# An FFT layer and a squared-relu FFN on one core: row d = 128 by a DMA, and P-Q+N moved to odd steps

## The chip, the core and the metric

The kernel runs on one NeuronCore of a Trainium2 chip. The metric is device time in microseconds for one execution. Before the change the median of three runs is 607.77 us (607.44 to 608.54). The engines are TensorE (PE in the profile, its weight loads PEld), VectorE (DVE), ScalarE (ACT), GpSimd (POOL) and SyncE (SP).

## The reference

```python
# x: 8 x 3008 x 256, w_in: 256 x 2048, w_out: 2048 x 256
X = np.fft.fft(x, axis=1)
X = np.fft.fft(X, axis=2)
a = X.real                      # 24064 rows of 256
h = np.maximum(a @ w_in, 0.0)
out = (h * h) @ w_out
```

## The kernel before

**Two outputs from one column.** The input is real, so the kernel transforms over the sequence only for the frequencies k up to half the sequence. For each such k it has a cosine part zc and a sine part zs (128 rows d, one column per k). With gh[:, 0] and gh[:, 1] (w_in after the transform over d) the hidden layer at k is relu of P+Q and the one at -k is relu of P-Q plus a small term N, where P comes from zc and Q from zs. N comes from one row alone, d = 128, which is kept in row 0 of zs: N for hidden unit f is that row times a number g2n[f].

**Windows and steps.** The 12040 columns are cut into 25 windows of up to 512 columns (`wins`; from window 6 on all have 512, the last, window 24, has 360). A window has 8 steps (`NST`), and a step makes 2 x 128 of the 2048 hidden units for all columns of the window, plus half (k) and minus half (-k), into h2. In the steps of window w also run: the second layer of window w-1 (16 matmuls of 256 columns per step, L687; the output copy osb, L702, comes in every odd step), the transform matmuls of the columns of window w+1 (`z_steps`, L572, spread over the steps lo to hi-1), and pieces of the input folds for a later batch (`at`, `post`: d_even, n_cos, d_odd, n_sin, even, away, odds, back, load, and the late pieces fold8, fold16, nyq8).

**Two forms of a step.** A *plain* step has four matmuls into a PSUM tile ph (`pq`, L829 and L830), the relu of the plus half on ScalarE (`first`, L861), the second-layer matmuls, two more matmuls with gh[:, 2] that turn P+Q into P-Q+N in place (`turn`, L852), and the relu of the minus half on ScalarE. VectorE squares both halves in one instruction (`power`, L868, 128x2048).

A *P-Q+N* step (the steps named in `diff`) saves the two `turn` matmuls: `cosines` (L838, two matmuls) makes P; VectorE computes t2 = N - 2P (`twice`, L842, scalar_tensor_tensor, called STT below); the second-layer matmuls run; `sines` (L847, two matmuls) makes P+Q in place and must wait for t2, since it writes the bank that t2 reads; ScalarE makes the relu of the plus half; VectorE adds t2 and ph with a saturating custom instruction (L859), which is the relu of the minus half. This instruction waits for ScalarE's relu of the same step. ScalarE squares the plus half (L872, issued after the relu of the next step), VectorE the minus half (L868, 128x1024).

**N.** n2 holds N for one P-Q+N step. `spread_nyq` brings row 0 of zs to all 128 partitions as zn: a matmul with a selector (`sel`, ones in row 0) into PSUM and a copy by ScalarE (L781, L782). `nyq_rows` makes n2 on GpSimd: per step two tensor_scalar instructions of 128x512 (L790). zn has two buffers. n2 has three (`wp`, tag w16), so the fourth set in order waits until the STT that reads the first has run.

**Order.** Everything is in an order written out by hand; each engine works its own instructions off in that order. Squares are not issued when they are ready: `keep` puts them in a list, and `settle` issues the list in the next step, after that step's `pq` or `twice`. `plus` does so for ScalarE's squares, after the relu of the next step. `held` keeps the transform's VectorE part (`apart`, L601) back, so that it does not come ahead of an STT. PSUM tile ph has two buffers, so step s+2 waits until both relus of step s have read theirs.

Before the change the P-Q+N steps are 0, 2, 4 and 6 in windows 6, 7, 11, 12, 14, 15, 17, 18 and 20 to 24; 2, 4 and 6 in windows 8, 10, 13, 16 and 19 (where the folds run in every step); 0 and 2 in window 9; 4 and 6 in windows 4 and 5. These are 73 steps. The row for window w+1 is spread in step `hi` of window w (5 or 6), and GpSimd makes the rows in that step and the next ones.

Of the kernel before, what the change touches and what calls it, by code (L numbers as in the profile page):

```python
# [9 lines left out]
F32 = mybir.dt.float32  # L10
F16 = mybir.dt.float16
I32 = mybir.dt.int32
AF = mybir.ActivationFunctionType
# [3 lines left out]
P = 128  # L17
# [3 lines left out]
def rev_dim(ap, i):  # L21

    dims = [list(d) for d in ap.ap]
    step, cnt = dims[i]
    dims[i] = [-step, cnt]
    return bass.AP(tensor=ap.tensor, offset=ap.offset + step * (cnt - 1), ap=dims)
# [3 lines left out]
def kernel(  # L30
# [14 lines left out]
    nc = tc.nc  # L45
    B, S, D = x.shape
# [33 lines left out]
    NW = len(wins)  # L80

    def win_of(col):
        return max(w for w in range(NW) if wins[w][0] <= col) if col < TOT else NW
# [5 lines left out]
    col_of = {}  # L89
# [11 lines left out]
    const = ctx.enter_context(tc.tile_pool(name="const", bufs=1))  # L101
# [12 lines left out]
    ps_z = ctx.enter_context(tc.tile_pool(name="ps_z", bufs=2, space=bass.MemoryType.PSUM))  # L114
# [35 lines left out]
    def load_rows(i):  # L150

        b, t = bs[i], xs[i]
        o = b * S * D
        if b == 0:
            nc.gpsimd.dma_start(out=t[0:1, 0, R - 1, :], in_=bass.AP(tensor=x.tensor, offset=x.offset + o, ap=[[D, 1], [1, D]]))
        if b + 1 == B:
            nc.gpsimd.dma_start(
                out=t[1:2, 2, :, :].rearrange("p c d -> p (c d)"),
                in_=bass.AP(tensor=x.tensor, offset=x.offset + o + (S - R) * D, ap=[[XW, 1], [1, XW]]))
# [156 lines left out]
    for i in (1, 0):  # L316
        nc.gpsimd.tensor_scalar(out=perm[i], in0=prow_i, scalar1=float(P - 1 - i), scalar2=None, op0=ALU.is_equal)
    nc.gpsimd.dma_start(out=wout16, in_=moe_w_out.rearrange("(c p) o -> p c o", p=P))
    sel = const.tile([P, P], F16, name="sel")
    nc.gpsimd.memset(sel, 0.0)  # L320
    nc.gpsimd.memset(sel[0:1, :], 1.0)
    pick = const.tile([P, 1], F16, name="pick")
    nc.gpsimd.memset(pick, 0.0)
    nc.gpsimd.memset(pick[0:1, :], -2.0)
# [213 lines left out]
    def zwin(w):  # L538
        if w not in zc:
            zc[w] = zp.tile([P, WN], F16, name="zc", tag="zc")  # L540
            zs[w] = zp.tile([P, WN], F16, name="zs", tag="zs")
        return zc[w], zs[w]

    held = {"on": False, "jobs": []}

    def let_go():
        jobs, held["jobs"] = held["jobs"], []
        for j in jobs:
            j()
# [81 lines left out]
    def run(*jobs):  # L631
        for j in jobs:
            j()
# [82 lines left out]
    def spread(jobs, i, n):  # L716
        return jobs[len(jobs) * i // n : len(jobs) * (i + 1) // n]
# [7 lines left out]
    NST = NFC // 2  # L725
    at_of = {w: [[] for _ in range(NST)] for w in range(NW)}
    post_of = {w: [[] for _ in range(NST)] for w in range(NW)}
    diff = {w: (0, 2, 4, 6) if w > 5 else (4, 6) for w in range(4, NW)}

    def put(w, s, i, name, *k, d=at_of):  # L730
        d[w][s].append(lambda: folds[i][name](*k))

    def late(w, s, i, *st):
        at_of[w][s].append(lambda: run(*[folds[i]["late"][k] for k in st]))

    def make(i):
        folds[i] = fold_steps(i)

    for i in range(2, B):
        b0 = (win_of(col_of[i, 0]) + win_of(col_of[i - 1, 1])) // 2 - 1  # L740
        tight = b0 - 2 in [(win_of(col_of[j, 0]) + win_of(col_of[j - 1, 1])) // 2 - 1 for j in range(2, i)]
        near = i == 2 or tight
        at_of[b0 - 1][0].append(lambda i=i: make(i))
        at_of[b0 - 2][7].append(lambda i=i: load_rows(i))
        put(b0 - 1, 5 if near else 2, i, "d_even", 0)
        put(b0 - 1, (6 if tight else 7) if near else 4, i, "d_even", 1)
        put(b0 if i == 2 else b0 - 1, 0 if i == 2 else 7 if near else 6, i, "n_cos")
        put(b0, 0, i, "d_odd", 0)
        put(b0, 1, i, "d_odd", 1)
        put(b0, 2, i, "n_sin")  # L750
        put(b0, 3, i, "even")
        put(b0, 4, i, "away")
        put(b0, 5, i, "odds")
        put(b0, 6, i, "back")
        put(b0, 6, i, "nyq", d=post_of)
        put(b0, 7, i, "load")
        for k, s in enumerate((3, 5, 6, 6)):
            late(b0 + 1, s, i, k)
        late(b0 + 2, 0, i, 4)
        if b0 > 5:  # L760
            diff[b0] = (2, 4, 6)
        if tight:
            diff[b0 - 1] = (0, 2)
    n2s = {}
    BIG = 3.0e38
    kept = []
    plus = []

    def settle():
        for k in kept:  # L770
            k()
        kept.clear()
        let_go()

    zns = {}

    def spread_nyq(wt):
        wn1 = wins[wt][1]
        zn = zns[wt] = znp.tile([P, WN], F16, name="zn", tag="zn")
        pn = ps_z.tile([P, 512], F32, name="pn", tag="pz")  # L780
        nc.tensor.matmul(pn[:, 0:wn1], sel, zwin(wt)[1][:, 0:wn1], start=True, stop=True)  # L781
        nc.scalar.activation(zn[:, 0:wn1], pn[:, 0:wn1], AF.Copy, bias=0.0, scale=1.0)  # L782

    def nyq_rows(wt, steps):
        wn1 = wins[wt][1]
        for s in steps:
            n2 = n2s[wt, s] = wp.tile([P, 2, WN], F32, name="n2", tag="w16")
            for a in range(2):
                fc = 2 * s + a
                nc.gpsimd.tensor_scalar(out=n2[:, a, 0:wn1], in0=zns[wt][:, 0:wn1], scalar1=g2n[:, fc : fc + 1], scalar2=1.0, op0=ALU.mult, op1=ALU.mult)  # L790

    old = None
    for w in range(NW):
# [1 line left out]
        h2 = h2p.tile([P, NFC, 2 * WN], F16, name="h2", tag="h2")  # L795
        zcw, zsw = zwin(w)

        lo, hi = int(any(win_of(col_of[i, 1]) == w + 1 for i in range(2, B))), NST - 3 if 0 in diff.get(w + 1, ()) else NST - 2
        at, post = at_of[w], post_of[w]
        if w == 1:  # L800
            fj = fold_jobs(1)
# [6 lines left out]
        elif w == 3:  # L808
# [4 lines left out]
            lo, hi = 3, NST - 1  # L813
        elif w == win_of(col_of[1, 1]) - 1:
            for st in range(5):
                at[min(st, 3)] += folds[1]["late"][st : st + 1]
            lo, hi = 4, NST - 1
# [36 lines left out]
        def relu(s, sg):  # L854
            h = h2[:, 2 * s : 2 * s + 2, sg * wn : (sg + 1) * wn]
            if sg:
                h = rev_dim(h, 2)
            if sg and s in t2s:
                nc.vector._custom_dve(TENSOR_ADD_SAT, out=h, in0=t2s[s][:, :, 0:wn], in1=phs[s][:, :, 0:wn], s0=BIG, s1=0.0)  # L859
            else:  # L860
                nc.scalar.activation(h, phs[s][:, :, 0:wn], AF.Relu, bias=0.0, scale=-1.0)  # L861

        def keep(*k):
            kept.append(lambda p=power: p(*k))

        def power(s, a, b, h2=h2, wn=wn):
            h = h2[:, 2 * s : 2 * s + 2, a * wn : b * wn]
            nc.vector.tensor_tensor(h, h, h, op=ALU.mult)  # L868
# [5 lines left out]
        def first(s):  # L874
            relu(s, 0)
            run(*plus)
            plus.clear()

        def others(s):
            for j in at[s]:  # L880
                j()
            for j in spread(f2, s, NST):
                j()
            for j in post[s]:
                j()
            if s == lo:
                zl[:] = [j for zu, part, h in zj for j in zu(part, h)]
            if s >= lo:
                for j in spread(zl, s - lo, hi - lo) if s < hi else []:
                    j()  # L890

        def nyq(s):
            if w + 1 in diff and hi < NST - 1:
                if s == hi:
                    spread_nyq(w + 1)
                    nyq_rows(w + 1, diff[w + 1][0:1])
                elif s == hi + 1:
                    nyq_rows(w + 1, diff[w + 1][1 : 2 if s < NST - 1 else None])
                elif s == hi + 2:
                    nyq_rows(w + 1, diff[w + 1][2:])  # L900
            if s == 0 and w in diff and w not in zns:
                spread_nyq(w)
                nyq_rows(w, diff[w])

        def quad(p):
            ph = phs[p] = ps_h.tile([P, 2, 512], F32, name="ph", tag="psh")
# [57 lines left out]
                keep(s1, int(s1 == NST - 1), 2)  # L964
            gh_nyq()
        for s in range(NST) if w > 1 else ():
            held["on"] = s + 1 in diff.get(w, ()) or (s + 1 == NST and 0 in diff.get(w + 1, ()))
            if s in diff.get(w, ()):
                cosines(s)
                twice(s)  # L970
                settle()
                others(s)
                sines(s)
                first(s)
                relu(s, 1)
                keep(s, 1, 2)
                plus.append(lambda s=s, p=power_act: p(s))
                nyq(s)
                continue
            pq(s)  # L980
            settle()
            first(s)
            if s == NST - 1:
                power(s, 0, 1)
            others(s)
            nyq(s)
            turn(s)
            relu(s, 1)
            keep(s, int(s == NST - 1), 2)
        if 0 not in diff.get(w + 1, ()):  # L990
            held["on"] = False
            settle()
        old = (w, h2)
    for j in ffn2_steps(*old, tail=True):
        j()
# [30 lines left out]
```

## Time and profile before

| | |
|---|---|
| median of three runs | 607.77 us |
| the profiled execution | 607.33 us, span 605.5 us |
| PE busy | 591.2 us, 98% |
| DVE busy | 490.1 us, 81% |
| ACT busy | 462.8 us, 76% |
| POOL busy | 213.6 us, 35% |
| selector matmul, L781 | 21, 379 ns each as the profile models it |
| copy to zn, L782 | 21, 616 ns mean with 512 columns |
| rows on POOL, L790 | 146, median 692 ns, up to 2444 |
| square of one half, L868 128x1024 | 107, mean 767 ns |
| square of both halves, L868 128x2048 | 73, mean 1284 ns |

All times are of one execution, counted from the start of its span. [...] Window 12 starts at 282.05, window 15 at 354.38, window 18 at 427.22, window 20 at 475.32, window 23 at 547.63, the last at 570.38.

### The profile page before, as it was taken

How to read it: one execution, taken by the hardware profiler on the slowest of the kernel's cores; microseconds unless marked ns; L12 is line 12 of the kernel's file. 1: busy time of each engine (PE TensorE's matmuls, PEld its weight loads, DVE VectorE, ACT ScalarE, POOL GpSimd, SP SyncE). 2: the span in 40 equal slices, each digit the busy share in tenths (PEclk: the TensorE clock that was granted, in tenths of full speed). 3: DMA queues.
4: the chain of work that ended last, by engine and by line, in shares of the span. 5: the costliest groups of instructions: out<-in, count | busy, mean ns of one | idle time of the engine just before them, and what ended most of it. 6: DMA issues, size and time to landing. Idle time of an engine off the chain costs nothing.

```text
span 605.5 us, 11294 instructions
## 1 busy us (share of the span) xinstructions
PE 591.2 (98%) x4449; PEld 427.9 (71%) x4449; DVE 490.1 (81%) x593; ACT 462.8 (76%) x634; POOL 213.6 (35%) x249
## 2 busy tenths in 40 slices
PE   7899999999999999999999999999999999999997
PEld 3457786776777777777777767777677777777786
DVE  8787656987998878979889799888988988777760
ACT  6697777968888787877787878787777787878762
POOL 8320223245504506365045451363431522513300
PEclk9999999999999999999999999999999999999999
DMA  8945321127111361271113711146112311111112
GB/s 150 155 90 136 115 71 34 39 94 150 52 49 40 114 140 52 77 166 48 52 37 109 146 53 36 40 125 134 44 30 86 88 35 39 51 46 38 54 57 69
DMA packets 36524, 47.52 MB, mean 78 GB/s; under 512 B 4215, under 2 KB 30327, under 8 KB 36471
## 3 DMA queue, kind: packets, MB, share of 16 engines
q0 software_dynamic: 9344, 22.14, 17.9%
q1 hardware_dynamic: 26899, 24.44, 13.5%
q8 instruction: 35, 0.57, 0.4%
q10 hardware_dynamic: 228, 0.21, 0.1%
q14 instruction: 18, 0.15, 0.1%
HBM read 33.63 MB, written 27.84 MB: 102 GB/s over the span
## 4 chain that ended last, share of the span: by engine, by line
PE 87%; DVE 9%; ACT 2%; issue 1%; POOL 0%; DVEq 0%; POOLq 0%; ACTq 0%
PE po L687 49%; PE ph L852 8%; PE ph L829 7%; PE ph L830 7%; PE ph L847 5%; PE ph L838 5%; PE pz L572 4%; DVE h L868 3%; DVE t L842 2%; DVE h L859 2%; DVE xy L491 1%; PE pn L781 1%; ACT h L923 1%; ACT h L861 0%; DVE m L243 0%
## 5 line engine op out<-in xcount | busy, mean ns | idle before, releaser
L687 PE MATMUL po<-wout,h 128*128 128x256 f16 (+1 forms) x3024 | 362.3, 273 | 0.0
L861 ACT ACTIVATE h<-ph 128x1024 f16<-128x1024 f32 (+3 forms) x311 | 295.5, 993 | 79.0 <-PE ph L847 59.1
L687 PEld LDWEIGHTS <-h 128*128 128x128 f16 (+1 forms) x3024 | 296.8, 98 | 72.0
L790 POOL TENSOR_SCALAR n<-zn,g2n 128x512 f32<-128x512 f16 (+2 forms) x146 | 144.2, 1002 | 256.3 <-ACT zn L782 248.4
L868 DVE TENSOR_TENSOR h<-h 128x1024 f16<-128x1024 f16 (+6 forms) x216 | 203.2, 951 | 30.0 <-ACT h L861 27.5
L859 DVE CUSTOM_DVE_ANT_0 h<-t,ph 128x1024 f16<-128x1024 f32 x67 | 81.7, 1220 | 31.6 <-ACT h L861 31.5
L842 DVE SCALAR_TENSOR_TENSOR t<-ph,n 128x1024 f32<-128x1024 f32 (+2 forms) x73 | 87.7, 1202 | 23.4 <-PE ph L838 22.1
L829 PE MATMUL ph<-zc,gh 128*128 128x512 f16 (+3 forms) x238 | 87.4, 368 | 0.4 <-ACT h L923 0.3
L830 PE MATMUL ph<-zs,gh 128*128 128x512 f16 (+3 forms) x238 | 87.4, 368 | 0.0
L872 ACT ACTIVATE h<-h 128x1024 f16<-128x1024 f16 (+2 forms) x73 | 76.5, 1048 | 0.0
L852 PE MATMUL ph<-zs,gh 128*128 128x512 f16 (+3 forms) x238 | 68.1, 368 | 0.2 <-ACT h L861 0.2
L702 ACT ACTIVATE osb<-po 128x512 f32<-128x512 f32 (+3 forms) x95 | 55.5, 589 | 10.6 <-PE po L687 9.7
L847 PE MATMUL ph<-zs,gh 128*128 128x512 f16 (+2 forms) x146 | 42.7, 374 | 1.4 <-DVE t L842 1.2
L838 PE MATMUL ph<-zc,gh 128*128 128x512 f16 (+2 forms) x146 | 42.8, 375 | 0.4 <-DVE h L859 0.4
L830 PEld LDWEIGHTS <-gh 128*128 128x128 f16 x238 | 23.2, 98 | 25.7 <-issue 0.9
L829 PEld LDWEIGHTS <-gh 128*128 128x128 f16 x238 | 23.2, 97 | 25.0
L577 ACT ACTIVATE es<-pz 128x376 f32<-128x376 f32 (+1 forms) x32 | 14.9, 486 | 16.4 <-PE pz L572 16.3
L852 PEld LDWEIGHTS <-gh 128*128 128x128 f16 x238 | 22.3, 98 | 6.2 <-issue 0.3
L838 PEld LDWEIGHTS <-gh 128*128 128x128 f16 x146 | 14.3, 98 | 17.2 <-issue 0.6
L456 POOL DMA_DIRECT2D scr<-ev x8 | 4.9, 616 | 58.3 <-DVE ev L452 52.5
L466 POOL DMA_INDIRECT rb<-scr,idx_r x16 | 18.2, 1140 | 4.9 <-issue 4.9
L132 POOL DMA_INDIRECT xo<-in_x_dram,idx_r x15 | 16.3, 1090 | 4.5 <-issue 4.3
(145 smaller groups left out, 368.5 us busy)
## 6 DMA issues: line engine op xcount, KB each, us to landing
out_dram<-osb SPq DMA_DIRECT2D x77, 128.0 KB
xo<-in_x_dram POOLq DMA_DIRECT2D x7, 768.0 KB
scr<-ev POOLq DMA_DIRECT2D x8, 390.0 KB, 2.9
rb<-scr POOLq DMA_DIRECT2D x16, 130.0 KB
out_dram<-osb SPq DMA_DIRECT2D x12, 94.0 KB
w<-in_moe_w_in_dram POOLq DMA_DIRECT2D x2, 512.0 KB
wout<-in_moe_w_out_dram POOLq DMA_DIRECT2D x1, 1024.0 KB, 11.9
out_dram<-osb SPq DMA_DIRECT2D x8, 75.0 KB
```

Of the source, the lines that this page charges most:

```text
L687: nc.tensor.matmul(po[0:m, j * D : (j + 1) * D], h2[:, fc, q : q + m], wout16[:, fc, :], start=(fc == 0), stop=(fc == NFC - 1))
L790: nc.gpsimd.tensor_scalar(out=n2[:, a, 0:wn1], in0=zns[wt][:, 0:wn1], scalar1=g2n[:, fc : fc + 1], scalar2=1.0, op0=ALU.mult, op1=ALU.mult)
L829: nc.tensor.matmul(ph[:, a, 0:wn], gh[:, 0, f0 : f0 + P], zcw[:, 0:wn], start=True, stop=False)
L830: nc.tensor.matmul(ph[:, a, 0:wn], gh[:, 1, f0 : f0 + P], zsw[:, 0:wn], start=False, stop=True)
L838: nc.tensor.matmul(ph[:, a, 0:wn], gh[:, 0, f0 : f0 + P], zcw[:, 0:wn], start=True, stop=True)
L842: nc.vector.scalar_tensor_tensor(out=t2[:, :, 0:wn], in0=phs[s][:, :, 0:wn], scalar=-2.0, in1=n2s[w, s][:, :, 0:wn], op0=ALU.mult, op1=ALU ...
L847: nc.tensor.matmul(phs[s][:, a, 0:wn], gh[:, 1, f0 : f0 + P], zsw[:, 0:wn], start=False, stop=True, skip_group_check=True)
L852: nc.tensor.matmul(phs[s][:, a, 0:wn], gh[:, 2, f0 : f0 + P], zsw[:, 0:wn], start=False, stop=True, skip_group_check=True)
L859: nc.vector._custom_dve(TENSOR_ADD_SAT, out=h, in0=t2s[s][:, :, 0:wn], in1=phs[s][:, :, 0:wn], s0=BIG, s1=0.0)
L861: nc.scalar.activation(h, phs[s][:, :, 0:wn], AF.Relu, bias=0.0, scale=-1.0)
L868: nc.vector.tensor_tensor(h, h, h, op=ALU.mult)
L872: nc.scalar.activation(h, h, AF.Square, bias=0.0, scale=1.0)
```

## The change

Row d = 128 is no longer spread by a matmul and a copy. ScalarE's DMA queue copies row 0 of zs, inside SBUF, to the 128 partitions of zn: one descriptor list of 128 times 1 KB. The selector and its two memsets go.

The P-Q+N steps become 1, 3, 5 and 7 where they were 0, 2, 4 and 6; 1 and 3 in window 9; 1, 3 and 5 in the last window. Windows 4, 5, 8, 10, 13, 16 and 19 keep theirs. There are 72 such steps instead of 73. Where step 7 is one, its plus half is squared on VectorE in that step (not on ScalarE), and its minus half in step 1 of the next window (`defer`).

The row is issued in step 4 or 5 (`hi`), where the transform matmuls of the next window have ended: these now take the steps 0 to hi-1. GpSimd makes one step's rows in each following step (one step later still in windows 5, 8, 10, 13, 16 and 19, where `back` is issued in step 6), and what is left in step 0 of the next window. d_even moves from steps 2 and 4 to 3 and 5, and the late fold pieces move from steps 3, 5, 6, 6 and 0 of the next window to 3, 4, 5, 5 and 6.

```diff
-    sel = const.tile([P, P], F16, name="sel")
-    nc.gpsimd.memset(sel, 0.0)
-    nc.gpsimd.memset(sel[0:1, :], 1.0)
...
-    diff = {w: (0, 2, 4, 6) if w > 5 else (4, 6) for w in range(4, NW)}
+    diff = {w: (4, 6) if w < 6 else (1, 3, 5) if w == NW - 1 else (1, 3, 5, 7) for w in range(4, NW)}
+    backs = []
...
+        backs.append(b0)
+        late(b0 + 1, 3, i, 0)
+        late(b0 + 1, 4, i, 1)
+        for k in (2, 3):
+            late(b0 + 1, 5, i, k)
+        late(b0 + 1, 6, i, 4)
+        put(b0 - 1, 5 if near else 3, i, "d_even", 0)
+        put(b0 - 1, (6 if tight else 7) if near else 5, i, "d_even", 1)
...
-            diff[b0 - 1] = (0, 2)
+            diff[b0 - 1] = (1, 3)
...
-        pn = ps_z.tile([P, 512], F32, name="pn", tag="pz")
-        nc.tensor.matmul(pn[:, 0:wn1], sel, zwin(wt)[1][:, 0:wn1], start=True, stop=True)
-        nc.scalar.activation(zn[:, 0:wn1], pn[:, 0:wn1], AF.Copy, bias=0.0, scale=1.0)
+        row = zwin(wt)[1][0:1, 0:wn1]
+        nc.scalar.dma_start(out=zn[:, 0:wn1], in_=bass.AP(tensor=row.tensor, offset=row.offset, ap=[list(row.ap[0]), [0, P], [1, wn1]]))
...
-        lo, hi = int(any(win_of(col_of[i, 1]) == w + 1 for i in range(2, B))), NST - 3 if 0 in diff.get(w + 1, ()) else NST - 2
+        lo, hi = 0, NST - 4 if 1 in diff.get(w + 1, ()) else NST - 3 if w + 1 in diff else NST - 2
...
+            if w + 1 in diff:
+                k = s - hi - int(w in backs)
                 if s == hi:
                     spread_nyq(w + 1)
+                elif s > hi and k > 0:
+                    nyq_rows(w + 1, diff[w + 1][k - 1 : k])
+            if s == 0 and w in diff:
+                nyq_rows(w, [q for q in diff[w] if (w, q) not in n2s])
...
                 settle()
+                if s == 1:
+                    run(*defer)
+                    defer.clear()
...
+                if s == NST - 1:
+                    power(s, 0, 1)
+                    relu(s, 1)
+                    defer.append(lambda p=power, s=s: p(s, 1, 2))
+                else:
+                    relu(s, 1)
+                    keep(s, 1, 2)
+                    plus.append(lambda s=s, p=power_act: p(s))
```

More of the change, by code (lines that the diff above doesn't have):

```diff
@@ L744 @@
         at_of[b0 - 2][7].append(lambda i=i: load_rows(i))
-        put(b0 - 1, 5 if near else 2, i, "d_even", 0)
-        put(b0 - 1, (6 if tight else 7) if near else 4, i, "d_even", 1)
+        backs.append(b0)
[6 more added lines that the diff above has]
+        put(b0 - 1, (6 if tight else 7) if near else 5, i, "d_even", 1)
         put(b0 if i == 2 else b0 - 1, 0 if i == 2 else 7 if near else 6, i, "n_cos")
@@ L756 @@
         put(b0, 7, i, "load")
-        for k, s in enumerate((3, 5, 6, 6)):
-            late(b0 + 1, s, i, k)
-        late(b0 + 2, 0, i, 4)
         if b0 > 5:
@@ L767 @@
     plus = []
+    defer = []
     def settle():
@@ L892, in nyq @@
         def nyq(s):
-            if w + 1 in diff and hi < NST - 1:
+            if w + 1 in diff:
+                k = s - hi - int(w in backs)
                 if s == hi:
                     spread_nyq(w + 1)
[L896 to L903, printed above, removed]
+                elif s > hi and k > 0:
+                    nyq_rows(w + 1, diff[w + 1][k - 1 : k])
+            if s == 0 and w in diff:
+                nyq_rows(w, [q for q in diff[w] if (w, q) not in n2s])
         def quad(p):
@@ L966 @@
         for s in range(NST) if w > 1 else ():
-            held["on"] = s + 1 in diff.get(w, ()) or (s + 1 == NST and 0 in diff.get(w + 1, ()))
+            held["on"] = s + 1 in diff.get(w, ())
             if s in diff.get(w, ()):
@@ L974 @@
                 first(s)
-                relu(s, 1)
-                keep(s, 1, 2)
-                plus.append(lambda s=s, p=power_act: p(s))
+                if s == NST - 1:
[6 more added lines that the diff above has]
+                    plus.append(lambda s=s, p=power_act: p(s))
                 nyq(s)
@@ L981 @@
             settle()
+            if s == 1:
+                run(*defer)
+                defer.clear()
             first(s)
@@ L989 @@
             keep(s, int(s == NST - 1), 2)
-        if 0 not in diff.get(w + 1, ()):
-            held["on"] = False
-            settle()
+        settle()
         old = (w, h2)
```

## The prediction

> **What bounds the kernel now.** I read the page's first part, then the chain of work in order of time, then the timeline of single engines around a step, then the places where TensorE was late.
>
> ```profile
> span 605.5 us, 11294 instructions
> PE 591.2 (98%) x4449; PEld 427.9 (71%) x4449; DVE 490.1 (81%) x593; ACT 462.8 (76%) x634; POOL 213.6 (35%) x249
> ```
>
> TensorE (PE) is busy 98% of the span. A modelled busy time could hide waits, so the chain is the better witness (columns: start, length, piece):
>
> ```profile
> 249.93 1.20 PE po L687 x11
> 251.13 0.21 PE pn L781
> 251.34 0.43 PE ph L852 x2
> 251.78 0.43 PE ph L838 x2
> 252.21 1.75 PE po L687 x16
> ```
>
> The matmuls stand end to end: 0.216 us for one of 512 columns, 1.75 for the sixteen of the second layer. So a P-Q+N step lasts 0.43 + 1.75 + 0.43 = 2.61 us, a plain step 0.87 + 1.75 + 0.43 = 3.05. The selector matmul (L781) is one link of this chain: whatever leaves TensorE here shortens the run.
>
> **Removed and added on TensorE.** The selector runs 21 times: 19 with 512 columns, one with 448, one with 360. 19 x 0.216 + 0.19 + 0.15 = 4.44 us gone, all on the chain. The last window has P-Q+N in three steps instead of four; such a step spares two matmuls of 360 columns, so 2 x 0.15 = 0.30 us come on. Elsewhere the number of such steps is unchanged.
>
> **Old waits that go.** Step 0 no longer has the form that waits for VectorE. What it cost is read in window 15 (step 0 from 354.38):
>
> ```profile
> 354.38 0.59 PE L838 MATMUL ph<-zc,gh 128*128 128x512 f16 x2
> 354.81 1.91 PE L687 MATMUL po<-wout,h 128*128 128x256 f16 x16
> 357.31 0.59 PE L847 MATMUL ph<-zs,gh 128*128 128x512 f16 x2 [0.59 <-DVE t L842]
> ```
> ```profile
> 354.31 1.81 DVE L868 TENSOR_TENSOR h<-h 128x1024 f16<-128x1024 f16 x2
> 356.05 1.21 DVE L842 SCALAR_TENSOR_TENSOR t<-ph,n 128x1024 f32<-128x1024 f32 x1
> ```
>
> The sines (L847) start 2.50 us after the second layer instead of 1.75: 0.75 lost. The same two rows give 0.17, 0.24, 0.74 and 0.24 in windows 7, 12, 18 and 21 (at 162, 284, 430, 503): 2.14 us together. VectorE came late because two squares of the window's last step lie ahead of P-Q+N there. In the new order step 0 has none, so these waits go; what is late next is step 7.
>
> **The new window boundary.** In 12 windows (6, 7, 11, 12, 14, 15, 17, 18, 20 to 23) step 7 becomes P-Q+N, and the square of its plus half must go on VectorE at once, ahead of the second relu. A light step in window 23 gives the times; let X be the start of the sines, 544.15:
>
> ```profile
> 544.78 1.94 ACT L861 ACTIVATE h<-ph 128x1024 f16<-128x1024 f32 x2 [1.02 <-PE ph L847]
> 547.55 0.60 ACT L702 ACTIVATE osb<-po 128x512 f32<-128x512 f32 x1
> 548.03 1.03 ACT L861 ACTIVATE h<-ph 128x1024 f16<-128x1024 f32 x1
> ```
> ```profile
> 545.84 1.22 DVE L859 CUSTOM_DVE_ANT_0 h<-t,ph 128x1024 f16<-128x1024 f32 x1 [0.48 <-ACT h L861]
> 547.09 1.30 DVE L868 TENSOR_TENSOR h<-h 128x1024 f16<-128x1024 f16 x2
> ```
>
> The relu starts at X + 0.63 and the custom add follows its end by 0.03. In step 7 the output copy (osb, odd steps) lies ahead: it starts 0.31 after the last second-layer matmul starts, X + 0.20, and the next activation 0.49 later, X + 0.69. Relu to X + 1.72; square from X + 1.75, next instruction 0.61 later (half of the x2 row); custom add X + 2.36 to X + 3.58. It frees the PSUM buffer that step 1 of the next window wants, and TensorE starts 0.055 after it (in window 20 at 482.08 to 482.14), X + 3.63. TensorE is there at X + 0.43 + 0.87 + 1.75 + 0.43 = X + 3.48. Lost: 0.16 us per boundary, 1.9 in all. This is the low end.
>
> GpSimd adds to it. There are three n2 buffers, so the third set of rows for the next window waits for step 7's STT (L842), which ends at X - 0.26; then two tensor_scalars run beside VectorE's squares. What such a meeting costs stands above: in the 354.31 row the two squares take 1.81 instead of 1.30, while GpSimd has
>
> ```profile
> 354.31 2.37 POOL L790 TENSOR_SCALAR n<-zn,g2n 128x512 f32<-128x512 f16 x2
> ```
>
> The square that comes into a running tensor_scalar waits for its end and then needs 0.55. Here the first tensor_scalar waits behind the full square of step 6 (X - 0.34 to X + 0.88) and ends near X + 1.43, the second near X + 2.10; the new square arrives at X + 1.75 and ends at X + 2.65 instead of X + 2.44. So 0.16 + 0.20 = 0.36 us per boundary, 12 x 0.36 = 4.3. I take this, because the buffer order makes them meet in every one of the 12.
>
> [...]
>
> **ScalarE.** 21 zn copies go (0.49 us each from one start to the next), 21 DMA issues come. Issues on this queue are in the tail, two in 0.81 us:
>
> ```profile
> 598.11 0.81 ACTq L667 DMA_DIRECT2D out_dram<-osb  x2
> ```
>
> I take 0.35. In step 4, counted from its first matmul: relu to 2.0, Square to 3.0, issue to 3.4, while relu of the minus half could start at 3.24. It is 0.2 us late; its square is not started before 4.9, its PSUM buffer not wanted before 5.66. Cost nothing; the cover is 0.4 us on VectorE's side, 1.2 on TensorE's. The issue also waits for VectorE's last part of zs (L601), which lies a step earlier. The high end is SyncE's row, 15 issues in 21.3 us, where the longest took 4.7; 14 of 311 took over 0.9. At that rate one of 21 costs 1 to 3 us.
>
> **Landing of the row.** Nearest: scr, 2.9 us; farthest: the indirect load, 11.4. The first rows are wanted in step 1 of the next window, about 11.7 us after the issue; two sets need 2.8 to 3.8. Hidden by 5 us at 2.9; at 11.4 late by 1 to 3 in each window (the less likely end: that row moves far more bytes).
>
> **The rest that moves.** The z steps end in step 3 instead of 4 or 5: same matmuls, their copies on ScalarE (0.49) now beside steps 0 to 3, whose plain ones lose the output copy (0.49). d_even moves a step later (0.97 on VectorE, two copies on ScalarE), each still in a P-Q+N step. fold8, fold16 and nyq8 come by step 6; 0.7 us in step 5 ends at 3.7 after the cosines, the relu that the custom add waits for at 3.9. GpSimd issues two scratch DMAs and two gathers in step 6, now ahead of the rows: 5 us of queue, rows wanted later than that. x loads and SyncE's stores keep their steps. The deferred square runs in step 1 and is wanted in step 4. One loss: n_cos (0.89) ahead of step 7's STT in windows 7, 12, 15 and 18 makes it about 0.1 late each, 0.4 in all; I set it against the 0.53 in window 20 that goes (next paragraph).
>
> **Sum.** -4.44 + 0.30 - 2.14 + 4.3 = -1.98 us on the profiled execution's 607.33 (span 605.5 and 1.8 around it): 605.35. The median of the runs, 607.77, stands 0.44 above that execution; so 605.8.
>
> **Rivals.** One, slower: GpSimd's burst starves the square. It has happened:
>
> ```profile
> 476.38 4.03 POOL L790 TENSOR_SCALAR n<-zn,g2n 128x512 f32<-128x512 f16 x6
> ```
> ```profile
> 477.17 3.79 DVE L868 TENSOR_TENSOR h<-h 128x1024 f16<-128x1024 f16 x1
> ```
>
> A square of 0.69 us took 3.79 because it came 0.1 us after a tensor_scalar started and lost to every following one, longer than one whole instruction; TensorE lost 0.53. In 350.57 and other bursts the square got in at the first end, so it depends on the phase. A late row makes such bursts just before step 7 (two sets, then the third). The mild form: the square comes just after the second tensor_scalar starts, waits 0.55 instead of 0.20, 0.71 us per boundary, 610.0 (0.12). The hard one: a further tensor_scalar gets ahead at each boundary, 12 x 0.67 = 8.0 us more than the forecast, 613.8 (0.10). It turns the sign from 0.17 us more per boundary on.
> Two, also slower: ScalarE held by its DMA issue, 21 x 0.4 over the cover: 614. For it, SyncE's long issues; against it, the short ones are 95%.
> Three, no change: the boundaries cost 0.36 and the steps with thin cover (0.2 to 0.4 us) give back 1 to 2 us more: 607.3.
> That the squares do not meet GpSimd (602.9 to 603.4) belongs to the forecast.
>
> **How the numbers follow.** A measurement of this kernel tells about 0.2% (1.2 us) from no change. Forecast 0.47 (602.3 to 606.5; at its low end all waits that the matmul starts show after 113 us are gone, 3.2 us, and a boundary costs 0.16), no change 0.20, GpSimd 0.22, ScalarE or a late row 0.11. Faster 0.47, same 0.20, slower 0.33. The range 602.3 to 612.5 leaves out 0.05 below and about 0.12 above.
>
> **What the new profile would show.** No L781 or zn copy; 4430 matmuls. Right: step 0 of windows 7, 12, 15, 18 and 21 lasts 3.05 us plus its z matmuls, and the first cosines after a P-Q+N step 7 wait 0.2 to 0.4 us on the custom add. Wrong: that wait nearer 1 us, squares above 1.3 us in step 7, ScalarE's issues above 0.9 us, or relus ending over 1.8 us after the sines start.

## The result and the profile after

| | before | after |
|---|---|---|
| median of six runs each | 607.89 us | 613.98 us (612.32 to 617.13) |
| ratio, 95% interval | | 1.010 (1.0083 to 1.0117) |
| the profiled execution, span | 607.33, 605.5 | 612.96, 611.2 |

The changed kernel is about 1% slower. The forecast was 605.8 with a range to 612.5: wrong in sign, and the time lies above the range. The page of the kernel after, its busy times, two of its DMA queues (packets, MB, share of the sixteen DMA engines) and its chain by engine:

```profile
span 611.2 us, 11237 instructions
PE 591.6 (97%) x4430; PEld 426.2 (70%) x4430; DVE 486.2 (80%) x591; ACT 445.8 (73%) x601; POOL 217.5 (36%) x245
...
q1 hardware_dynamic: 26899, 24.44, 13.1%
q10 hardware_dynamic: 3252, 2.91, 11.9%
...
PE 76%; DVE 11%; ACT 6%; issue 3%; DMA 2%; POOL 1%; SPq 0%; POOLq 0%; ACTq 0%; DVEq 0%
```

The same lines of the page before:

```profile
q1 hardware_dynamic: 26899, 24.44, 13.5%
...
q10 hardware_dynamic: 228, 0.21, 0.1%
...
PE 87%; DVE 9%; ACT 2%; issue 1%; POOL 0%; DVEq 0%; POOLq 0%; ACTq 0%
```

The 21 selector matmuls are gone. But TensorE carries 76% of the chain where it carried 87%, and queue 10 (ScalarE's) moves 2.91 MB in 11.9% of the engines' time, while queue 1 (SyncE's stores) needs 13.1% for 24.44 MB. So a row costs 0.118 x 16 x 611.2 / 21 = 55 us of engine time, 3.4 us of all sixteen.

The largest single loss is in the chain of the kernel after in window 11 (start, length, piece):

```profile
274.18 0.45 PE ph L853 x2
...
274.65 1.03 ACT h L862
275.68 1.19 SPq L664
...
276.92 1.20 SPq L664
...
278.16 3.07 DMA out_dram<-osb
281.23 0.03 ACT osb L699
...
281.72 1.95 ACT h L862 x2
...
283.70 1.01 PE ph L853 x2
284.71 0.85 PE ph L839 x2
285.57 2.38 PE po L684 x16
```

The output copy on ScalarE (L699) waits for an output buffer whose store has not landed; the relu behind it on the same engine waits with it; TensorE, which wants the relu's result, stands idle for 3.81 us.

Which store it was, the chain only infers, and the one it names (issued at 278.16) does not fit. The three output buffers take turns, so the copy at 281.22 needs the stores of the copy at 257.26. SyncE issued these from 259.07 to 260.68, and the semaphore of the last of them counts its last arrival at 281.06, 20.4 us after the issue. Before, the same store was issued at 258.99 and its last arrival counted at 268.76.

Then a pair of matmuls takes 1.01 and 0.85 us instead of 0.43, and the second layer 2.38 instead of 1.75. Two stretches of the same execution (busy time and count of PE, PEld, DVE, ACT and POOL; granted clock; DMA share; GB/s), the stretch of those slow matmuls and the one behind it:

```profile
283.60:286.60 3.00, 2.90 (x10) 1.43 (x10) 2.16 (x5) 2.02 (x3) 0.00 (x0) 0.50 0.17 52
286.60:290.00 3.40, 3.40 (x27) 2.44 (x25) 1.91 (x3) 2.02 (x3) 2.26 (x2) 0.98 0.11 39
```

The granted clock was 0.50 for 3 us after the gap: 0.58 + 0.42 + 0.63 = 1.6 us more on the same matmuls.

What filled the DMA engines there? The x load of a later sample fills them from 265 to 270 in both kernels (share 1.06 before, 1.02 after). The next ten microseconds in the same view, of the kernel before and then of the kernel after:

```profile
270.00:275.00 5.00, 5.00 (x38) 3.53 (x37) 4.50 (x8) 3.71 (x8) 0.00 (x0) 1.00 0.40 107
275.00:280.00 5.00, 5.00 (x38) 3.43 (x36) 4.83 (x7) 3.91 (x6) 2.71 (x3) 1.00 0.20 63
```
```profile
270.00:275.00 5.00, 5.00 (x38) 3.39 (x36) 4.96 (x10) 4.15 (x7) 1.94 (x2) 1.00 0.84 150
275.00:280.00 5.00, 4.89 (x39) 3.59 (x37) 3.45 (x5) 0.68 (x1) 0.00 (x0) 1.00 0.78 68
```

From 275 to 280 the engines are 78% busy and move hardly more than before with 20%: busy, but not with bytes. (In the five before that the x load is part of it: GpSimd issued it at 263.0 instead of 259.7, behind the scratch gather.) The row was issued at 272.74.

But the late store was issued 12 us before that row. It had an earlier row ahead of it, issued at 248.63: beside its packets two of SyncE's issues took 3.45 and 2.48 us. At 263.85, when the x load is about to begin, 134 packets of stores had been issued and not begun, against 35 at the same point before (counted in the packet records). Then came the x load, in which one issue of SyncE took 7.15 us from 266.24 on, with no row in flight, and then the row of 272.74. How much of the 20 us each of them made is not separated here. The waits of the kernel after that end in a transfer or follow from one (sum, times, longest):

```profile
POOL rb L461 <- DMA scr<-ev: 38.9, 7, 10.1
...
ACT osb L699 <- DMA out_dram<-osb: 10.5, 5, 5.5
DVE t L843 <- POOL n L791: 7.7, 3, 3.6
```

Before, the first was 2.7, the second 0.3 and the third 0.5, each once.

Where the 5.7 us between the two spans lie, by the starts of the first matmul of each step against matmuls back to back (0.2165 us from one start to the next for 512 columns; the profile shows each of them with 0.379 us, so only starts are compared), from window 4 on. "Late" is what a step lasts beyond that.

| late, us | before | after |
|---|---|---|
| sines of step 0 wait for VectorE (windows 7, 12, 15, 18, 21) | 2.23 | 0 |
| steps 6 and 7 of window 11 (the stall above) | 0 | 5.48 |
| first cosines after a P-Q+N step 7 (12 boundaries) | 0 | 2.76 |
| step 7 of windows 7, 12, 15, 18 (n_cos ahead of it) | 0 | 0.95 |
| step 6 of windows 10, 13, 16, 19 | 0 | 1.00 |
| step 1 of window 11 and other single waits of windows 6 to 22 | 1.23 | 3.5 |
| window 4, and all below 0.05 | 4.2 | 3.9 |
| sum | 7.65 | 17.6 |

10.0 more late, 4.44 - 0.30 less of matmuls: 5.8 us, against 5.7 between the spans.

### The profile page after: what moved, and what is told of

It reads as the page before. It is cut to its first block, busy times and chain, and to the rows that moved or that the text cites. A ratio compares the mean times of both kernels' runs of the same rounds, so it can differ in the third digit from the quotient of the medians.

```text
span 611.2 us, 11237 instructions
## 1 busy us (share of the span) xinstructions
PE 591.6 (97%) x4430; PEld 426.2 (70%) x4430; DVE 486.2 (80%) x591; ACT 445.8 (73%) x601; POOL 217.5 (36%) x245
## 3 DMA queue, kind: packets, MB, share of 16 engines
q1 hardware_dynamic: 26899, 24.44, 13.1%
q10 hardware_dynamic: 3252, 2.91, 11.9%
## 4 chain that ended last, share of the span: by engine, by line
PE 76%; DVE 11%; ACT 6%; issue 3%; DMA 2%; POOL 1%; SPq 0%; POOLq 0%; ACTq 0%; DVEq 0%
PE po L684 43%; PE ph L853 7%; PE ph L830 7%; PE ph L831 6%; PE ph L848 4%; PE ph L839 4%; PE pz L569 3%; ACT h L862 3%; DVE h L860 2%; DVE h L869 2%; DVE t L843 2%; DMA scr<-ev 2%; ACT h L921 1%; DMA out_dram<-osb 1%; DVE zc L598 1%
## 5 line engine op out<-in xcount | busy, mean ns | idle before, releaser
L869 DVE TENSOR_TENSOR h<-h 128x2048 f16<-128x2048 f16 (+6 forms) x216 | 204.0, 955 | 39.2 <-ACT h L862 35.6
L791 POOL TENSOR_SCALAR n<-zn,g2n 128x512 f32<-128x512 f16 (+2 forms) x144 | 147.3, 1037 | 234.9 <-DMA zn<-zs 177.6
L699 ACT ACTIVATE osb<-po 128x512 f32<-128x512 f32 (+3 forms) x95 | 55.1, 584 | 72.5 <-PE po L684 56.3
L873 ACT ACTIVATE h<-h 128x1024 f16<-128x1024 f16 (+2 forms) x60 | 63.0, 1050 | 0.0
L461 POOL DMA_DIRECT2D rb<-scr x16 | 8.8, 552 | 47.1 <-DMA scr<-ev 38.9
## 6 DMA issues: line engine op xcount, KB each, us to landing
wout<-in_moe_w_out_dram POOLq DMA_DIRECT2D x1, 1024.0 KB, 11.9
```

The costliest lines, as they stand in the source:

```text
L873: nc.scalar.activation(h, h, AF.Square, bias=0.0, scale=1.0)
```

## The experiments

The theory after this reading (T1): the row's DMA itself costs the time, because its 128 packets all come out of one SBUF partition and hold the DMA engines, so that stores and the scratch copy land late. Rivals: the new order of the steps costs it (T2, with GpSimd's meetings as its mechanism), or the issue on ScalarE's queue does (T3). The expectations call T1 theory D and T2 theory O. All ratios are to runs of the kernel before on the same chip.

**The selector back in the new order.** On the kernel after:

```diff
-        row = zwin(wt)[1][0:1, 0:wn1]
-        nc.scalar.dma_start(out=zn[:, 0:wn1], in_=bass.AP(...))
+        pn = ps_z.tile([P, 512], F32, name="pn", tag="pz")
+        nc.tensor.matmul(pn[:, 0:wn1], sel, zwin(wt)[1][:, 0:wn1], start=True, stop=True)
+        nc.scalar.activation(zn[:, 0:wn1], pn[:, 0:wn1], AF.Copy, bias=0.0, scale=1.0)
```

> The new order, with the selector matmul and the copy to zn put back in place of the DMA. Theory D (the row's DMA is what costs: it fills the DMA engines for 5 us a window, stores land late, the output copy waits for its buffer): the waits of 0.3 us and more around the output copy go (5.5 us in the profiled execution), the selector costs its 4.4 us again; the rest of the new order's waits stay. So 610 to 612, and a spread between runs under 1 us instead of 4.8. Theory O (the new order costs, at the boundary between windows): 612.96 + 4.4 less nothing, 616 to 617, same spread as before.

616.38 us, 1.0135 (1.0119 to 1.015). This seemed to speak for T2, but the trace has a cost of the edit's own. The waits of this kernel have a line that the others lack, TensorE's selector held up behind ScalarE:

```profile
PE pn L786 <- ACT h L866: 4.5, 4, 1.1
```

In windows 10, 13, 16 and 19 the row is not ready where the new order issues it; a DMA can wait there, but a matmul stops TensorE, 1.3 us each, 5.2 in all. So this run isn't a clean control; a later one repairs that.

**The row's DMA alone, in the kernel before.** The selector stays, and a second copy of the row goes by the change's own DMA, from the same place and queue, into a tile that nobody reads:

```diff
+        zx = zxp.tile([P, WN], F16, name="zx", tag="zx")
+        row = zwin(wt)[1][0:1, 0:wn1]
+        nc.scalar.dma_start(out=zx[:, 0:wn1], in_=bass.AP(tensor=row.tensor, offset=row.offset, ap=[list(row.ap[0]), [0, P], [1, wn1]]))
```

> The kernel before, with the row's DMA in addition, into a tile that nobody reads, issued by ScalarE right after the selector's copy. Theory D: 2 to 6 us slower than before, with output copies that wait for their stores. Theory O: within 0.2% of before (607.9), since the order is the old one. If ScalarE's issue is what costs, 21 x 0.35 us of its time, slower by up to 3 us, but then the plain copy beside it costs the same.

613.55 us, 1.0096 (1.0081 to 1.0111): 5.3 us for a transfer whose result nothing uses. Its profiled execution loses 4.2 us in steps 4 and 5 of window 11, where another output copy waits for a store, and the next row comes only after that:

```profile
276.69 0.60 ACT L703 ACTIVATE osb<-po 128x512 f32<-128x512 f32 x1 [3.89 <-DMA out_dram<-osb]
...
283.46 0.48 ACTq L786 DMA_DIRECT2D zx<-zs  x1
```

The row before it was issued at 254.55, and its packets were over by 261.5. So a row does harm beyond its own packets: it leaves stores waiting, and the x load finds them there (176 packets at 266.87, where one issue of SyncE then took 8.04 us). A second place is steps 6 and 7 of window 6, 1.8 us later than before: the row's issue on ScalarE's queue stands behind a store that landed at 156.98, and a relu behind the issue.

**The same bytes from 128 partitions.** As the last, with one other line:

```diff
+        nc.scalar.dma_start(out=zx[:, 0:wn1], in_=zwin(wt)[1][:, 0:wn1])
```

> The kernel before, with a DMA of the same size on the same queue at the same place, but from 128 partitions to 128 partitions instead of from one row. Theory D in its form that 128 packets out of one partition are slow (480 ns against 46 ns for a store's packet of the same 1 KB): within 0.2% of before. If it is the issue on ScalarE or the number of bytes: as slow as with the row's DMA.

608.33 us, 1.0003 (0.9994 to 1.0012): nothing. The queue lines of the two kernels, the row first:

```profile
q10 hardware_dynamic: 3252, 2.91, 12.0%
```
```profile
q10 hardware_dynamic: 3252, 2.91, 1.5%
```

Equal packets, equal bytes, eight times the time. In the packet records a 1 KB packet of a row takes 485 ns (median) and one of a store or of the plain copy 46; a full row's packets lie over 4.8 to 8.1 us in the kernel after. SyncE's issues show what that does to the stores (ns min, median, max; kernel with the row, then with the plain copy):

```profile
L668 SPq DMA_DIRECT2D out_dram<-osb x311: 228/355/8044, 40.8 to 607.7; - x156
```
```profile
L668 SPq DMA_DIRECT2D out_dram<-osb x311: 228/346/5002, 40.4 to 600.8; - x156
```

The median issue hardly changes; the longest grows from 5.0 to 8.0 us, and 51 of the 311 take over 0.9 us where 15 did. ScalarE's own issue takes the same time in both (0.47 and 0.48 us, 21 times), so T3 falls. Why a packet out of one partition takes 485 ns is not shown.

**Six output buffers in the kernel after.** If the stall of window 11 is a store's buffer, more buffers remove it and leave the late rows:

```diff
-    osp = ctx.enter_context(tc.tile_pool(name="osp", bufs=3))
+    tmm = ctx.enter_context(tc.tile_pool(name="tmm", bufs=1))
+    osp = ctx.enter_context(tc.tile_pool(name="osp", bufs=6))
...
-            m = st["m", h] = tmp.tile([P, 3, NE], F32, name="m", tag="tm")
+            m = st["m", h] = tmm.tile([P, 3, NE], F32, name="m", tag="tm")
```

> The changed kernel with six output buffers instead of three (room for them comes from one buffer less of a table tile that only the first 60 us use). Theory D in its form that the copy waits for a buffer whose store has not landed: 607 to 609, no wait of the output copy on a store, spread under 2 us. If the row's DMA hurts in another way, or theory O: 612 to 614 as the changed kernel.

610.27 us, 1.0041 (1.0028 to 1.0055), 3.7 below the kernel after. Its waits:

```profile
POOL rb L462 <- DMA scr<-ev: 39.1, 7, 10.5
...
DVE t L844 <- POOL n L792: 7.9, 3, 3.6
...
ACT osb L700 <- DMA out_dram<-osb: 1.2, 1, 1.2
```

The output copy's wait fell from 10.5 to 1.2 and window 11 has no stall; the rows are as late as they were. The late stores are the larger part of the row's price. From window 4 on this execution loses 5.4 us less than the kernel after did; but its window 4 starts at 94.20 instead of 91.54, and the room for the buffers came from a table tile of the first 60 us. So 3.7 may be too little for the stores; that part is not separated.

**The row over DRAM.** A DMA out of one partition once, then a DRAM row read 128 times, both on GpSimd's queue:

```diff
-        nc.scalar.dma_start(out=zn[:, 0:wn1], in_=bass.AP(tensor=row.tensor, ...))
+        hop = drp.tile([1, WN], F16, name="hop", tag="hop")
+        nc.gpsimd.dma_start(out=hop[:, 0:wn1], in_=row)
+        nc.gpsimd.dma_start(out=zn[:, 0:wn1], in_=bass.AP(tensor=hop.tensor, offset=hop.offset, ap=[[0, P], [1, wn1]]))
```

> The changed kernel, but the row goes by two DMAs of GpSimd's queue: row 0 of zs to 1 KB of DRAM, and from there to the 128 partitions, so that no 128 packets come out of one SBUF partition. Theory D (packets of 480 ns out of one partition fill the DMA engines; stores and the scratch copy land late): packets under 100 ns, no output copy that waits for a store, scratch copy back to 2.7 us, 606 to 608, spread under 2 us. If any second-layer store is late because of the number of DMAs or bytes, 612 to 614 as the changed kernel.

608.48 us, 1.0002 (0.9991 to 1.0013): 5.5 below the kernel after, with the same order and no selector. The same ten microseconds as above:

```profile
270.00:275.00 5.00, 5.00 (x40) 3.69 (x38) 4.64 (x8) 3.85 (x7) 2.05 (x4) 1.00 0.99 212
275.00:280.00 5.00, 5.00 (x38) 3.46 (x37) 4.96 (x8) 3.70 (x5) 0.58 (x1) 1.00 0.21 58
```

The x load is over by 275 and no stall follows. With the extra row (+5.3) and this (-5.5) the price of the row's DMA stands from both sides, and T1 holds for the larger part of the loss. What is left: 4.1 us of matmuls are gone on balance, and the time is that of before. So something else in the change costs about as much.

**A fourth n2 buffer.** The prediction's mechanism for the boundary was GpSimd's rows waiting for one of three buffers. On the last kernel, with the table's own pool as above, and:

```diff
-    wp = ctx.enter_context(tc.tile_pool(name="wp", bufs=3))
+    wp = ctx.enter_context(tc.tile_pool(name="wp", bufs=4))
```

> As the two-hop kernel, with four n2 buffers instead of three (room from one table buffer less, which costs up to 2 us in the first 60 us). GpSimd then need not wait for the STT of step 7 before it makes the third set of rows, and does not meet the square of step 7. My prediction's term: the boundary (excess of step 0 after a P-Q+N step 7) falls from 0.2 or 0.3 us to 0.16 or less, 1 to 2 us over the run. If GpSimd plays no part in it: the same excess as with three buffers.

611.82 us, 1.0062 (1.0037 to 1.0086). The boundaries cost 3.99 against 3.61 without it, and one of them alone 1.43, where a square of both halves lost to four tensor_scalars in a row and took 3.2 us. More buffers move the meetings, they don't remove them.

**The old order with the row over DRAM.** The kernel before without its selector, the two DMAs one step earlier:

```diff
-        pn = ps_z.tile([P, 512], F32, name="pn", tag="pz")
-        nc.tensor.matmul(pn[:, 0:wn1], sel, ...)
-        nc.scalar.activation(zn[:, 0:wn1], pn[:, 0:wn1], ...)
+        hop = drp.tile([1, WN], F16, name="hop", tag="hop")
+        nc.gpsimd.dma_start(out=hop[:, 0:wn1], in_=zwin(wt)[1][0:1, 0:wn1])
+        nc.gpsimd.dma_start(out=zn[:, 0:wn1], in_=bass.AP(tensor=hop.tensor, ...))
```

> The old order (P-Q+N in 0, 2, 4 and 6) without the selector, the row by the same two DMAs, spread one step earlier. If the row's only fault is the slow packets, and the new order costs 3 us beside it: 603.5 to 605 (607.9 less 4.4 for the selector). If the old order needs the row sooner than two DMAs bring it: waits of the STT for n2 in step 0, and 606 or more.

626.07 us, 1.0289 (1.0269 to 1.0309). Step 0 is P-Q+N in this order and has no rows yet when it starts:

```profile
DVE t L842 <- POOL n L790: 22.0, 9, 5.4
...
PE ph L847 <- DVE t L842: 17.6, 8, 5.1
```

So the order isn't a whim beside the DMA: with the old one a row that comes over DRAM is too late, 18 us of TensorE's waiting. Whether the change's single DMA would be in time in the old order was not run.

**The order alone.** The selector in the new order again, one step later, where its row is ready:

```diff
-                if s == hi:
+                if s == min(hi + 1, NST - 1):
                     spread_nyq(w + 1)
-                elif s > hi and k > 0:
+                if s > hi and k > 0:
```

> The new order with the selector matmul one step later than in the first experiment (step 5 or 6, as in the kernel before), where zs is ready. The first experiment's 1.30 us in step 4 of windows 10, 13, 16 and 19 should go, 5.2 us in all: 611 to 612, so that the order alone costs about 3 us against before. If those 1.30 us come from the order itself: 616 again.

611.35 us, 1.004 (1.0028 to 1.0052): the order costs 2.9 us. One of its boundaries, window 11 to 12 (X, the sines of step 7, at 284.01), on ScalarE, VectorE, GpSimd and TensorE:

```profile
284.21 0.60 ACT L702 ACTIVATE osb<-po 128x512 f32<-128x512 f32 x1 [1.15 <-PE po L687]
284.70 1.94 ACT L866 ACTIVATE h<-ph 128x1024 f16<-128x1024 f32 x2
```
```profile
283.67 1.22 DVE L873 TENSOR_TENSOR h<-h 128x2048 f16<-128x2048 f16 x1
285.75 0.90 DVE L873 TENSOR_TENSOR h<-h 128x1024 f16<-128x1024 f16 x1 [0.86 <-ACT h L866]
286.57 1.21 DVE L864 CUSTOM_DVE_ANT_0 h<-t,ph 128x1024 f16<-128x1024 f32 x1
```
```profile
283.85 2.26 POOL L795 TENSOR_SCALAR n<-zn,g2n 128x512 f32<-128x512 f16 x2 [0.26 <-DVE t L847]
```
```profile
287.83 0.59 PE L843 MATMUL ph<-zc,gh 128*128 128x512 f16 x2 [0.19 <-DVE h L864]
```

Relu at X + 0.69, the square of step 6 from X - 0.34 to X + 0.88, the new square from X + 1.74 to X + 2.64 beside two tensor_scalars that end at X + 2.10, the custom add from X + 2.56, the next cosines at X + 3.82: the prediction's schedule was X + 0.69, X - 0.34 to X + 0.88, X + 1.75 to X + 2.65, X + 2.57 and X + 3.84. All twelve boundaries of this kernel are late, by 0.09 to 0.58; 3.7 us in all.

**The square split.** TensorE needs only the first 128 columns of the new square at once; the custom add can come before the rest. On the kernel with the row over DRAM:

```diff
                 if s == NST - 1:
-                    power(s, 0, 1)
+                    square(s, 0, P)
                     relu(s, 1)
+                    square(s, P, wn)
```

> The two-hop kernel, with step 7's square of the plus half cut in two: the 128 columns that the next window's first group reads, then the custom add, then the other 384. By the boundary arithmetic the custom add starts 0.36 us (0.61 less 0.25) earlier, at X + 2.0 without GpSimd, ends at X + 3.2, and TensorE at X + 3.48 no longer waits; with GpSimd in front of the small square up to 0.2 us of wait stays. The excess of step 0 after a P-Q+N step 7, 3.6 us in all with two hops, falls under 1 us: 605.5 to 606.5. If the waits there come from something other than the square in front of the custom add: 608.5 as before.

606.29 us, 0.9963 (0.995 to 0.9975): 2.2 below the same kernel without the split; the twelve boundaries cost 0.5 us instead of 3.6. Another 1.4 us went in step 0 of window 20, which follows a plain step 7: there VectorE's squares met six tensor_scalars of GpSimd in a row, and the second layer waited for them.

**And n_cos off step 6.** With the split, n_cos of the four windows where the prediction charged 0.1 each moves from step 6 to step 7:

```diff
-        put(b0 if i == 2 else b0 - 1, 0 if i == 2 else 7 if near else 6, i, "n_cos")
+        put(b0 if i == 2 else b0 - 1, 0 if i == 2 else 7, i, "n_cos")
```

> As the run with the split square, and n_cos (0.89 us on VectorE, windows 7, 12, 15 and 18) moved from step 6, where it lies ahead of step 7's STT, into step 7, where VectorE is idle between the full square and the relu's end. If the 0.93 us of waits at the end of step 7 in these windows come from it, 0.7 to 1.0 us faster than the run with the split square alone; if they come from GpSimd or from ScalarE, no difference.

604.99 us, 0.9944 (0.9926 to 0.9963): the best, faster than both kernels. The 0.93 us at the end of step 7 are gone from its profile; so is the 1.4 of window 20, which the edit does not explain, and the interval overlaps that of the split alone, so the edit's own worth is not measured. Its boundary from window 22 to 23 (X at 544.55), VectorE and TensorE:

```profile
544.21 1.21 DVE L871 TENSOR_TENSOR h<-h 128x2048 f16<-128x2048 f16 x1
546.29 0.29 DVE L875 TENSOR_TENSOR h<-h 128x256 f16<-128x256 f16 x1 [0.87 <-ACT h L864]
546.50 1.22 DVE L862 CUSTOM_DVE_ANT_0 h<-t,ph 128x1024 f16<-128x1024 f32 x1
547.63 0.64 DVE L875 TENSOR_TENSOR h<-h 128x768 f16<-128x768 f16 x1
```
```profile
548.02 0.59 PE L841 MATMUL ph<-zc,gh 128*128 128x512 f16 x2
```

The custom add starts at X + 1.95 instead of X + 2.56, and the cosines at X + 3.47 without a wait.

**The same two edits with the change's DMA.** On the kernel after, both edits above:

> The changed kernel with its own DMA of the row (one DMA on ScalarE's queue, out of one partition), the split square and n_cos in step 7. Beside e10 this differs in the row's way alone. If the row's DMA costs what it cost in the other pairs (extra row against before 5.3 us, changed kernel against two hops 5.5), 610 to 611.5, with a spread of 2 us or more. If its cost came from the tight boundary that it met, 606 to 607.

610.9 us, 1.0038 (1.0025 to 1.0052): 5.9 above the last kernel, for the row's DMA alone. In the profiled executions (here its slowest, 612.26), where its steps are 7.8 us later, 7.1 of that lie in steps 1, 6 and 7 of window 11. So nearly all the price comes from one place, where the x load follows a row whose delayed stores are still waiting (137 packets at 265.03, against 39 at the same point of the last kernel) and the next row follows the x load; the other rows cost little in this order.

**The same two edits with the selector.** On the kernel with the selector one step later:

> The new order with the selector one step later, the split square and n_cos in step 7: beside e10 it differs in the selector alone, which TensorE pays with 4.4 us. If these come off in full where nothing else waits, 609 to 609.5. If VectorE is the limit in the steps where the selector stood (its 0.216 us are slack for VectorE), the difference is nearer 3 us: 607.5 to 608.5.

607.94 us, 0.9997 (0.9987 to 1.0007): 3.0 above the version over DRAM, though its selector takes 4.44 us. Step 6 of windows 10, 13, 16 and 19 tells why in part: 0.25 us late each in the versions of the new order without the selector, on time in this one and in the one with the late selector alone. TensorE comes to VectorE's part of that step sooner and waits for it, so 1.0 us of the saving is given back. In the two profiled executions window 4 starts 0.7 us apart the other way, about what that start differs between executions of other pairs; whether that belongs to the edit isn't settled.

## Why the prediction was wrong

**Removed and added on TensorE: right in size, not in worth.** The matmuls lost 4.44 us and gained 0.30, as worked out. Two pairs of kernels that differ only in how the row is spread, by the selector (one step later) or over DRAM, give 2.9 (611.35 to 608.48) and 3.0 us (607.94 to 604.99). "Whatever leaves TensorE here shortens the run" was too strong: some steps had less slack on VectorE than the selector took.

**Old waits that go: right.** 2.23 us in windows 7, 12, 15, 18 and 21, none after.

**The new window boundary: right in mechanism, somewhat large.** The schedule holds to 0.02 us where it could be read, but not every boundary meets it: 2.8 us after, 3.7 with the selector, 4.3 forecast. That late rows shift some meetings away in the kernel after is argued, not shown.

**ScalarE's issue: right at zero.** 0.48 us each instead of 0.35, and the plain copy shows that this is covered (in the old order). The rival that had ScalarE held by its issue falls, though its 614 is what came out.

**Landing of the row: the step that failed.** It asked when the row arrives and bounded that by two other transfers' landings. It did not ask what the row does to the rest: the DMA engines were a resource that the sum did not hold. The row's lateness was the small part. The large one is 3.4 us of all sixteen engines per row, in front of SyncE's stores; the stores then still wait when the x load comes, and from there it goes by the output buffers to ScalarE and TensorE. +5.3, -5.5 and +5.9 us in three comparisons. The profile of before listed no transfer of this kind, so its price had to be bounded above and zero was no bound; and the store that waits was named only as unchanged ("x loads and SyncE's stores keep their steps"). That the scratch copy's readers wait (38.9 us in all, up to 10.1) is for the most part the new order: with the selector in it they wait 31.0 in all, up to 6.9.

**The rest that moves: too small.** n_cos cost 0.95 us, not 0.4; step 6 of four windows 1.0, not foreseen. Window 20's wait (0.55) did go.

**In sum:** forecast -2.0, found +5.8 by the table. Of the 7.8 between them the stall of window 11 makes 5.5, n_cos and the other single waits 3.2 (the forecast set n_cos against window 20's wait and had none of the others), step 6 of four windows 1.0; the boundaries take back 1.5 and the small rest 0.4. The version with n_cos moved still has 1.7 of the single waits, so about half of them belong to the order, not to the row. By the runs' times: the order +2.9, the selector's end -2.9, the row's DMA +5.5.

**The rivals.** GpSimd's burst did not decide it: no boundary of the kernel after lost more than 0.58 us. That its hard form gave 613.8, near the measured time, is luck. A burst was seen with four n2 buffers (1.43) and in step 0 of window 20 with the split square (1.4).

Open: the runs of the kernel after spread from 612.3 to 617.1, more than any other; only one was profiled, so which further stalls the longer ones had isn't known. That other rows can stall as well shows in window 6 of the kernel with the extra row, not in the kernel after.

## What to carry to other kernels

A DMA has two prices, when it lands and what it keeps from moving: take its engines' time, bytes and source partitions into the sum, and look at which transfers wait behind it and what comes next on the same engines. Here a row to be spread over all partitions went better over DRAM than 128 times out of one partition (608.48 against 613.98 us). When an instruction between two engines costs a wait, ask which part of its output the next engine needs first, and do only that part ahead.

## What the runs showed of the hardware beyond that

- A 1 KB packet out of one partition's row took 485 ns (median) in the kernel after, a 1 KB packet of a store 46. Other queues were delayed: of SyncE's 311 issues 14 took over 0.9 us before and 41 after. One of the 41, of 7.15 us from 266.24 on, came when the row's packets had been over since 257.8.
- TensorE idle for 3.8 us was followed by 3 us at a granted clock of 0.50, which added 1.6 us to the stall (the kernel after). In the kernel with the extra row 2.4 us without a matmul (276.33 to 278.70) were followed by 3.3 us at 0.50: the matmuls from 278.70 to 283.12 lasted 4.42 us instead of 2.62.
- VectorE's square lost to four GpSimd instructions in a row with four n2 buffers (3.2 us for one of 1.2). In the kernel before, one of 0.69 us took 3.79 beside a burst of six. Having lost to one, it lost to the next as well.
